# One batch's q transposed on TensorE instead of by DMA, the last quarter stored in two halves, and new instruction lists

## The chip, the core and the metric

The kernel runs on one NeuronCore of one Trainium2 chip. The time is device microseconds of one execution: 237.6 us is the median of three runs of the kernel before, which lie between 237.46 and 240.7 us. The profiled execution took 238.53 us, of which the span of its instructions is 236.7 us; the other 1.83 us lie outside the span.

## The reference

Eight batches of attention in two steps, followed by a gated MLP:

```python
s = scale * q k^T;  a = exp(s - max) / sum          # sm_attn(qq, kk, vv)
p_packed = sm_attn(p, k, v)          # 32 packed queries per head over 576 keys
out      = sm_attn(q, p_packed, p_packed)   # 576 queries over the 32 packed keys
x = out as (8*576, 8*64)
h = x @ w_in                          # 512 -> 2048
g = h * sigmoid(beta * h)
return g @ w_out                      # 2048 -> 512
```

Shapes: q, k, v (8, 8, 576, 64), p (8, 8, 32, 64), w_in (512, 2048), w_out (2048, 512), output (4608, 512), all float32 outside; the kernel computes in bfloat16 with float32 sums.

## The kernel before

The work goes batch by batch (b = 0 to 7). For each batch q, k and v are loaded by SyncE's queue, cast to bfloat16, and k and q are transposed, since both are contracted over the head dimension. In batches 0 and 1 (`PE_BATCHES = 2`) the transposes run on TensorE into PSUM (`tp`, L424) and VectorE or ScalarE copy them out (L585, L587, L608, L610); from batch 2 on one DMA transpose per tensor (L597) writes kT and qT directly, once all three casts of the tensor are done.

Then come the first scores (`s1`, `s1r`) and their exponential, the packed values (`pun`, tile `pp_ps`), the second scores (`s2`), exponential, sum over 32 keys (`z2`), its inverse by log and exp on ScalarE (`l2`, `n2`), and the weights `A2T` on VectorE (L890). The packed values are multiplied with w_in (`w`, tile `w_ps`), scaled by beta on VectorE (`W_bf`, L950 and L957). The hidden layer is then `h` = W_bf times A2T, two matmuls of 512 columns for each of 16 slices of the hidden dimension, then silu on ScalarE (`g_main`, L992). The 64 leftover tokens of a batch (576 = 512 + 64) go into `hr` and are collected over four batches in `g_rem`.

The last product is `o`: for batch 0 plain, 64 pairs of 512-column matmuls; for the others by a scheme with seven products of half-size blocks in place of eight (`plan_seven`, `seven`): four sums of g on VectorE (`S`, tile `g_sum`, L1223), seven products `p`/`P` of 16 matmuls with 256 columns each, reads `R11` to `R22+` from PSUM into `o_sb` (L1253, L1255), and stores (L1155). The sums of w_out blocks that it needs (`T4`, tile `w_sum`, L1133) are made once, after all of w_out is there.

Loads at the start share one ring of three staging buffers: w_in 0 to 3, w_out 0 to 3 and the packed queries p of batches 2 to 7 (L1414) go through it, and each must wait until the casts from the buffer's previous tenant are done. p is cast on POOL (L1418) and transposed on TensorE (`p_tr`, tile `pT_ps`), ahead of the first scores of batch 2.

What sets the order: five written lists (`SEQUENCE`, L84), one for each engine, give the order of all tasks; a table `HOME` says which PSUM ring some early tiles take. `Planner.run` walks these lists with assumed durations only to decide which engine's next task is emitted and how many filler matmuls (`keep_warm`, L438: 128x128 on a matrix of ones) stand before a TensorE task in the first 60 us. Each engine's order is then fixed in the program, and the engines wait for each other by semaphores alone. Where one TensorE instruction waits, all behind it wait.

Of the kernel before, what the change touches and what calls it, by code (L numbers as in the profile page):

```python
# [25 lines left out]
TS = 9  # L26
# [36 lines left out]
HOME = {  # L63
    ("bcol",): "att",
    ("brow", 0): "att",
    ("brow", 1): "att",
    ("brow", 3): "att",
    ("tr", 0, "k", 0): "h",
    ("trr", 0, "k"): "h",
    ("tr", 0, "q", 0): "h",  # L70
    ("tr", 0, "q", 1): "h",
    ("s1r", 0): "h",
    ("z2", 0, 1): "h",
    ("z2", 0, 2): "h",
    ("w", 0, 0): "h",
    ("w", 0, 2): "h",
    ("tr", 1, "k", 0): "h",
    ("trr", 1, "q"): "h",
    ("s1r", 1): "h",
    ("z2", 1, 0): "h",  # L80
    ("w", 1, 0): "h",
# [1470 lines left out]
```

## Time and profile before

| What | Value |
|---|---|
| median of 3 runs | 237.6 us (237.46 to 240.7) |
| profiled execution, its span | 238.53 us, 236.7 us |
| TensorE busy | 226.3 us (96%), 2642 matmuls |
| VectorE, ScalarE, POOL busy | 158.5 us, 169.6 us, 70.9 us |
| granted TensorE clock | full speed in all 40 slices |
| chain that ended last | 75% TensorE, 14% DMA |

The page's busy shares are means over the span; a row of a window tells what is busy in one stretch. In the chain of waits, each piece is what released the next one. In the timeline a number in brackets is the engine's idle time before the instruction, followed by what ended it.

### The profile page before, as it was taken

How to read it: one execution, taken by the hardware profiler on the slowest of the kernel's cores; microseconds unless marked ns; L12 is line 12 of the kernel's file. 1: busy time of each engine (PE TensorE's matmuls, PEld its weight loads, DVE VectorE, ACT ScalarE, POOL GpSimd, SP SyncE). 2: the span in 40 equal slices, each digit the busy share in tenths (PEclk: the TensorE clock that was granted, in tenths of full speed). 3: DMA queues.
4: the chain of work that ended last, by engine and by line, in shares of the span. 5: the costliest groups of instructions: out<-in, count | busy, mean ns of one | idle time of the engine just before them, and what ended most of it. 6: DMA issues, size and time to landing. Idle time of an engine off the chain costs nothing.

```text
span 236.7 us, 6282 instructions
## 1 busy us (share of the span) xinstructions
PE 226.3 (96%) x2642; PEld 157.4 (67%) x2668; DVE 158.5 (67%) x255; ACT 169.6 (72%) x312; POOL 70.9 (30%) x84
## 2 busy tenths in 40 slices
PE   7999999969999999999999999999999999999993
PEld 7668743334577656865688557776685667777882
DVE  3755989688689627965786877913885657644661
ACT  2548889748799877985779669797898688665200
POOL 3557316411854052046108420813305000000000
PEclk9999999999999999999999999999999999999999
DMA  6999999999998899999999999799893340031313
GB/s 227 395 387 399 395 395 332 280 333 221 275 274 170 238 250 204 284 295 252 254 280 342 203 290 242 186 295 214 166 322 58 60 172 8 4 136 44 82 54 133
DMA packets 67108, 54.16 MB, mean 229 GB/s; under 512 B 38948, under 2 KB 58532, under 8 KB 66568
## 3 DMA queue, kind: packets, MB, share of 16 engines
q1 hardware_dynamic: 67072, 53.75, 84.6%
q8 instruction: 21, 0.34, 0.6%
q14 instruction: 7, 0.06, 0.1%
q10 hardware_dynamic: 8, 0.01, 0.0%
HBM read 37.23 MB, written 9.44 MB: 197 GB/s over the span
## 4 chain that ended last, share of the span: by engine, by line
PE 75%; DMA 14%; SPq 2%; DVE 2%; POOL 2%; ACT 1%; issue 1%; POOLq 0%; ACTq 0%
PE o_ps L419 44%; PE h_ps L419 19%; DMA w_in<-in_moe_w_in_dram 5%; DMA w_out<-in_moe_w_out_dram 5%; PE hr_ps L419 3%; DMA v<-in_v_dram 3%; PE w_ps L419 3%; PE s_ps L419 2%; DMA k<-in_k_dram 2%; PE pp_ps L419 1%; PE z_ps L419 1%; POOL w_in_bf L1458 1%; SPq L483 1%; DVE g_main L1223 1%; SPq L490 1%
## 5 line engine op out<-in xcount | busy, mean ns | idle before, releaser
L992 ACT ACTIVATE g_main<-h_ps 128x512 bf16<-128x512 f32 x128 | 71.1, 595 | 32.4 <-PE h_ps L419 23.6
L419 PEld LDWEIGHTS <-g_main 128*128 128x128 bf16 x624 | 59.0, 98 | 22.0 <-issue 3.2
L419 PE MATMUL h_ps<-A2T,W_bf 128*128 128x512 bf16 x235 | 65.5, 379 | 0.7 <-issue 0.2
L419 PE MATMUL o_ps<-w_out_bf,g_main 128*128 128x256 bf16 (+1 forms) x395 | 59.9, 289 | 1.0 <-DVE o_sb L1255 0.5
L419 PEld LDWEIGHTS <-W_bf 128*128 128x128 bf16 x512 | 32.6, 98 | 19.5 <-issue 3.7
L950 DVE TENSOR_TENSOR W_bf<-w_ps,beta_bc 128x512 bf16<-128x512 f32 x48 | 30.5, 683 | 11.0 <-PE w_ps L419 10.8
L419 PE MATMUL o_ps<-w_sum,g_sum 128*128 128x256 bf16 x256 | 34.3, 273 | 0.1
L419 PE MATMUL o_ps<-w_sum,g_main 128*128 128x256 bf16 x224 | 30.4, 273 | 0.2
L436 ACT ACT_TABLE_LOAD x22 | 28.2, 1283 | 1.1 <-PEq L1536 0.7
L1253 DVE TENSOR_TENSOR o_sb<-o_ps,o_sb 128x512 f32<-128x512 f32 (+1 forms) x27 | 17.0, 629 | 17.9 <-PE o_ps L419 15.1
L419 PEld LDWEIGHTS <-g_sum 128*128 128x128 bf16 x256 | 24.0, 98 | 7.1 <-issue 1.7
L515 POOL CAST v_bf<-v 128x1024 bf16<-128x1024 f32 x12 | 15.3, 1296 | 40.5 <-DMA v<-in_v_dram 35.7
L515 POOL CAST q_bf<-q 128x1024 bf16<-128x1024 f32 x12 | 13.6, 1150 | 28.2 <-DMA q<-in_q_dram 15.7
L1255 DVE COPY o_sb<-o_ps 128x512 f32<-128x512 f32 (+1 forms) x21 | 13.1, 624 | 10.6 <-PE o_ps L419 8.7
L1255 ACT COPY o_sb<-o_ps 128x512 f32<-128x512 f32 (+1 forms) x15 | 8.2, 546 | 15.3 <-PE o_ps L419 15.3
L515 POOL CAST k_bf<-k 128x1024 bf16<-128x1024 f32 x12 | 13.2, 1123 | 13.2 <-DMA k<-in_k_dram 6.6
L419 PE MATMUL o_ps<-ones 128*128 128x128 bf16 x176 | 14.5, 238 | 1.1 <-DVE ones L1302 1.1
L419 PEld LDWEIGHTS <-ones 128*128 128x128 bf16 x176 | 12.2, 108 | 3.1 <-issue 1.2
L957 DVE SCALAR_TENSOR_TENSOR W_bf<-w_ps,rz,beta_bc 128x512 bf16<-128x512 f32 x16 | 11.3, 742 | 1.8 <-PE w_ps L419 1.6
L890 DVE TENSOR_TENSOR A2T<-E2T,rz 128x512 bf16<-128x512 bf16 x16 | 11.2, 709 | 0.6 <-ACT rz L885 0.6
L1223 DVE TENSOR_TENSOR g_sum<-g_main 128x2048 bf16<-128x2048 bf16 x7 | 8.8, 1256 | 3.3 <-ACT g_main L992 3.3
L419 PE MATMUL w_ps<-w_in_bf,pp 64*32 64x512 bf16 x256 | 10.7, 382 | 0.1
(124 smaller groups left out, 269.7 us busy)
## 6 DMA issues: line engine op xcount, KB each, us to landing
k<-in_k_dram SPq DMA_DIRECT2D x6, 1024.0 KB, 8.9
v<-in_v_dram SPq DMA_DIRECT2D x6, 1024.0 KB, 8.2
q<-in_q_dram SPq DMA_DIRECT2D x6, 1024.0 KB, 8.8
out_dram<-o_sb SPq DMA_DIRECT2D x10, 512.0 KB, 4.5
w_in<-in_moe_w_in_dram SPq DMA_DIRECT2D x4, 1024.0 KB, 11.5
w_out<-in_moe_w_out_dram SPq DMA_DIRECT2D x4, 1024.0 KB, 11.1
out_dram<-o_sb SPq DMA_DIRECT2D x12, 256.0 KB, 4.5
k<-in_k_dram SPq DMA_DIRECT2D x4, 576.0 KB, 5.8
```

Source lines behind the costliest of these rows:

```text
L419: return self.nc.tensor.matmul(out, lhsT, rhs, start=start, stop=stop, tile_position=pos, skip_group_check=True)
L436: self.nc.scalar.preload_act_table_set(SETS[mode])
L483: nc.sync.dma_start(t[64 * g : 64 * g + 64, :].rearrange("p (h d) -> p h d", h=4), src[b, 4 * g : 4 * g + 4, SM:S, :].rearrange("h p d -> ...
L490: nc.sync.dma_start(t[:].rearrange("p (i e f) -> p i e f", i=2, e=2)[:, i], src[b].rearrange("(e i a) (s t) d -> i (a s) e (t d)", e=2, i= ...
L515: self.copy[engine](o[:, 0 : 32 * e].rearrange("p (t h e) -> p h t e", t=4, h=8)[:, h, :, 0:D], t[:, 0:2048].rearrange("p (h t d) -> p h t ...
L890: nc.vector.tensor_tensor(part(st[b, "A2"], i), part(st[b, "E2"], i), st[b, "rz2"][:, i] if i < 2 else st[b, "rz2r"][:], ALU.mult)
L950: nc.vector.tensor_tensor(st[b, "W"][:, r, cols].rearrange("q (f p) -> q f p", f=4), st[b, "w", m][:].rearrange("q (p f) -> q f p", f=4), ...
L957: nc.vector.scalar_tensor_tensor(st[b, "W"][:, r, cols].rearrange("q (f p) -> q f p", f=4), st[b, "w", m][:].rearrange("q (p f) -> q f p", ...
L992: nc.scalar.activation(st[b, "g"][:, ft, :], st[b, "h", ft][:], AF.Silu)
L1223: nc.vector.tensor_tensor(o, x, y, op)
L1253: nc.vector.tensor_tensor(o, x, o, ALU.add)
L1255: self.copy[engine](o, x)
```

## The change

Three edits, and all five lists written anew. q of batch 2 is transposed on TensorE (`ON_PE`), by two sets of eight and one of two 128x128 transposes with three copies out of PSUM; its DMA transpose goes away. In the last unit the last quarter of the output (`R21`) is read and stored by halves of its tokens: the first half does not wait for the last group of matmuls. Beside the order itself, the lists give 15 tasks from ScalarE to VectorE and 16 the other way; eight casts and one cross copy (`pn` of batch 0) leave POOL for VectorE or ScalarE, and one cross copy comes to it (`pn` of batch 1).

```diff
 PE_BATCHES = 2
+ON_PE = ((2, "q"),)
 ...
 HOME = {
+    ("p0_tr",): "h",
 ...
-        return [("pun", b)] if x == "v" else [("tr", b, x, 0), ("tr", b, x, 1)] + [("trr", b, x)] * (b < PE_BATCHES)
+        return [("pun", b)] if x == "v" else [("tr", b, x, 0), ("tr", b, x, 1)] + [("trr", b, x)] * (b < PE_BATCHES or (b, x) in ON_PE)
 ...
-                a = 128 * (TS * i + t)
+                a = 128 * ((TS if b < PE_BATCHES else 8) * i + t)
 ...
-            if x == "k":
+            if x == "k" or b >= PE_BATCHES:
 ...
-                a = 128 * (TS * u + 8)
+                a = 128 * (TS * u + 8 if b < PE_BATCHES else 16 + u)
 ...
-            if b >= PE_BATCHES:
+            if b >= PE_BATCHES and (b, x) not in ON_PE:
 ...
-            for row, col in ((0, 0), (1, 1), (0, 1), (1, 0)):
+            for m in range(2):
+                self.task(("store", n + 1, 0, m), "SP", 0.36, lambda m=m: store(1, 0, slice(m, m + 1)), [c["21"][m]], -10)
 ...
+            for row, col in ((0, 0), (1, 1), (0, 1)):
 ...
-        c21 = R("21", [p4, r22], ends=[one])
+        if b == B - 1:
+            c21 = [
+                self.task(
+                    ("R21", b, m), {"DVE": 0.38, "ACT": 0.28}, None, lambda e, m=m: read("21", e, m),
+                    [p4 if m else ("p", b, 4, 2), r22], base + 5, ends=[one] if m else (),
+                )
+                for m in range(2)
+            ]
+        else:
+            c21 = R("21", [p4, r22], ends=[one])
```

SyncE's queue, the loads behind those of batch 0. Before (the k of the first line is batch 1's, k_732 batch 2's, and the p near the end holds the packed queries of batches 2 to 7):

```order
L490 DMA k_215<-in_k_dram 128x2x576 x2
L1452 DMA w_in_238<-in_moe_w_in_dram 128x4x512
L1452 DMA w_in_247<-in_moe_w_in_dram 128x4x512
L1462 DMA w_out_253<-in_moe_w_out_dram 128x2048
L1452 DMA w_in_634<-in_moe_w_in_dram 128x4x512
L1452 DMA w_in_727<-in_moe_w_in_dram 128x4x512
L475 DMA k_732<-in_k_dram 128x8x256
L483 DMA k_732<-in_k_dram 64x4x64 x2
L1462 DMA w_out_836<-in_moe_w_out_dram 128x2048
L1414 DMA p_865<-in_p_dram 96x1024
L1462 DMA w_out_916<-in_moe_w_out_dram 128x2048
```

Now (the first line is the first w_in; q_789 and k_888 belong to batch 2):

```order
L1465 DMA w_in_176<-in_moe_w_in_dram 128x4x512
L489 DMA k_216<-in_k_dram 128x2x576 x2
L1465 DMA w_in_237<-in_moe_w_in_dram 128x4x512
L489 DMA q_312<-in_q_dram 128x2x576 x2
L1475 DMA w_out_357<-in_moe_w_out_dram 128x2048
L1465 DMA w_in_613<-in_moe_w_in_dram 128x4x512
L1465 DMA w_in_778<-in_moe_w_in_dram 128x4x512
L474 DMA q_789<-in_q_dram 128x8x256
L1475 DMA w_out_846<-in_moe_w_out_dram 128x2048
L1427 DMA p_871<-in_p_dram 96x1024
L474 DMA k_888<-in_k_dram 128x8x256
L1475 DMA w_out_926<-in_moe_w_out_dram 128x2048
```

The first w_in stands ahead of k of batch 1 instead of behind it, each load of w_in by itself; q of batch 2 has taken the place of k of batch 2, and k of batch 2 stands behind p and ahead of the last w_out.

VectorE around the first scaled weights of batch 0 (`W_bf`, the first SCALAR_TENSOR_TENSOR). Before:

```order
L610 COPY kT<-krT_ps 128x256
L608 COPY qT<-qrT_ps 128x2x2x64
L585 COPY kT<-kT_ps 128x1024
L890 TENSOR_TENSOR A2T<-E2T,rz_458 128x512
L957 SCALAR_TENSOR_TENSOR W_bf<-w_ps,rz_364,beta_bc 128x512 x2
L890 TENSOR_TENSOR A2T<-E2T,rz_458 128x512
L1469 TENSOR_SCALAR w_out_bf<-w_out_253,rbeta 128x512
L957 SCALAR_TENSOR_TENSOR W_bf<-w_ps,rz_364,beta_bc 128x512
```

Now:

```order
L607 COPY qT<-qrT_ps 128x2x2x64
L1413 COPY beta_bc<-brow_ps 128x512
L776 COPY pp<-px 64x64 x2
L530 CAST k_bf<-k_216 128x2x9x64
L956 SCALAR_TENSOR_TENSOR W_bf<-w_ps,rz_359,beta_bc 128x512 x2
L584 COPY kT<-kT_ps 128x1024
L889 TENSOR_TENSOR A2T<-E2T,rz_469 128x512 x2
L609 COPY kT<-krT_ps 128x256
L584 COPY kT<-kT_ps 128x1024
L1471 CAST w_in_bf<-w_in_237 128x2x512
```

The cross copy of the packed values (`pp<-px`) and a cast of k of batch 1 have come from POOL and stand ahead of the first W_bf; the transposed k of batch 1 (`kT`) is copied out behind it instead of ahead of it, and a cast of w_in has come in.

TensorE around the transposes of p (`pT_ps`, eight of them; the first and the last are shown). Before:

```order
L419 LDWEIGHTS W_bf
L419 MATMUL h_ps<-A2T,W_bf 128x512
L424 LDWEIGHTS p_865
L424 MATMUL pT_ps<-identr,p_865 128x96
...
L424 LDWEIGHTS p_865
L424 MATMUL pT_ps<-identr,p_865 128x96
L419 LDWEIGHTS W_bf
L419 MATMUL h_ps<-A2T,W_bf 128x512
...
L419 LDWEIGHTS ones
L419 MATMUL o_ps<-ones 128x128
```

Now:

```order
L418 LDWEIGHTS W_bf
L418 MATMUL h_ps<-A2T,W_bf 128x512
L418 LDWEIGHTS g_main
L418 MATMUL o_ps<-w_out_bf,g_main 128x512
L418 LDWEIGHTS g_main
L418 MATMUL o_ps<-w_out_bf,g_main 128x512
L423 LDWEIGHTS p_871
L423 MATMUL pT_ps<-identr,p_871 128x96
...
L423 LDWEIGHTS p_871
L423 MATMUL pT_ps<-identr,p_871 128x96
L418 LDWEIGHTS W_bf
L418 MATMUL h_ps<-A2T,W_bf 128x512
```

Ahead of these transposes stand now 22 pairs of h matmuls instead of 19, 17 pairs of o matmuls instead of 15, the two new sets of eight q transposes, and all 170 fillers (before: 164 ahead, 12 behind, 176 in all); the first pair of o that reads the ninth and tenth slice of w_out stands ahead of them, too.

## Rows read from the trace of the kernel before

**Rows 1.** the page's part 1, busy time, share and instructions of each engine.

```profile
PE 226.3 (96%) x2642; PEld 157.4 (67%) x2668; DVE 158.5 (67%) x255; ACT 169.6 (72%) x312; POOL 70.9 (30%) x84
```

**Rows 2.** the page's part 4, shares of the chain that ended last.

```profile
PE 75%; DMA 14%; SPq 2%; DVE 2%; POOL 2%; ACT 1%; issue 1%; POOLq 0%; ACTq 0%
```

**Rows 3.** stretches: start:end, length, each engine's busy time (instructions), clock, DMA share, GB/s.

```profile
45.00:50.00 5.00, 2.84 (x13) 1.08 (x11) 3.06 (x7) 2.77 (x5) 1.06 (x2) 1.00 0.98 285
...
25.00:45.00 20.00, 19.63 (x214) 9.11 (x216) 18.95 (x35) 17.52 (x29) 8.36 (x8) 1.00 1.07 359
...
60.00:233.00 173.00, 170.97 (x2004) 124.03 (x2022) 114.64 (x171) 128.18 (x236) 45.27 (x51) 1.00 0.80 194
...
22.82:64.01 41.19, 38.52 (x374) 19.66 (x378) 34.22 (x57) 32.38 (x58) 17.07 (x18) 1.00 1.08 323
```

**Rows 4.** timeline: start, us, engine, line, operation, out<-in, idle before <-releaser.

```profile
37.82 0.36 SPq L1414 DMA_DIRECT2D p<-in_p_dram  x1
...
48.94 1.04 POOL L1418 CAST p<-p 96x1024 bf16<-96x1024 f32 x1 [3.92 <-DVE W_bf L957]
...
50.04 0.51 PE L424 MATMUL pT_ps<-identr,p 96*128 96x96 bf16 x8 [2.19 <-POOL p L1418]
...
51.25 1.28 DVE L1469 TENSOR_SCALAR w_out_bf<-w_out,rbeta 128x512 bf16<-128x512 f32 x3 [0.39 <-DMA w_out<-in_moe_w_out_dram]
```

**Rows 5.** issues on SyncE's queue: KB each, median us to landing.

```profile
p<-in_p_dram SPq DMA_DIRECT2D x1, 384.0 KB, 11.0
```

**Rows 6.** pieces of the chain: start, us, what.

```profile
8.33 11.36 DMA w_in<-in_moe_w_in_dram
...
19.81 2.49 POOL w_in_bf L1458 x2
...
28.09 0.45 PE qT_ps L424 x8
...
53.38 0.43 PE o_ps L419 x2
```

**Rows 7.** timeline, a run of fillers on TensorE.

```profile
23.06 1.18 PE L419 MATMUL o_ps<-ones 128*128 128x128 bf16 x18
```

**Rows 8.** timeline, VectorE's first W_bf and first sum of g.

```profile
22.82 1.41 DVE L957 SCALAR_TENSOR_TENSOR W_bf<-w_ps,rz,beta_bc 128x512 bf16<-128x512 f32 x2 [1.42 <-PE w_ps L419]
...
64.01 1.29 DVE L1223 TENSOR_TENSOR g_sum<-g_main 128x2048 bf16<-128x2048 bf16 x1
```

**Rows 9.** timeline, VectorE operations of the kinds added or removed.

```profile
19.98 0.69 DVE L585 COPY kT<-kT_ps 128x1024 bf16<-128x1024 bf16 x1 [0.17 <-PE kT_ps L424]
...
20.59 0.81 DVE L890 TENSOR_TENSOR A2T<-E2T,rz 128x512 bf16<-128x512 bf16 x1
...
19.32 0.29 DVE L610 COPY kT<-krT_ps 128x256 bf16<-128x256 bf16 x1 [0.98 <-PE krT_ps L424]
...
36.20 0.69 DVE L1458 CAST w_in_bf<-w_in 128x1024 bf16<-128x1024 f32 x1
...
30.98 0.76 DVE L531 CAST v_bf<-v 128x1152 bf16<-128x1152 f32 x1 [0.18 <-DMA v<-in_v_dram]
...
24.92 0.48 DVE L1469 TENSOR_SCALAR w_out_bf<-w_out,rbeta 128x512 bf16<-128x512 f32 x1
...
34.01 0.38 DVE L777 COPY pp<-px 64x64 bf16<-64x64 bf16 x2
...
54.73 0.56 DVE L1426 COPY pT<-pT_ps 64x384 bf16<-64x384 bf16 x1
```

**Rows 10.** timeline of ScalarE, a table load and what follows it.

```profile
34.17 1.28 ACT L436 ACT_TABLE_LOAD   x1
...
35.47 1.26 ACT L849 ACTIVATE E2T<-s_ps,rz 128x512 bf16<-128x512 f32 x2
```

**Rows 11.** timeline, ScalarE's reads of output blocks near the end.

```profile
219.91 0.37 ACT L1255 COPY o_sb<-o_ps 128x256 f32<-128x256 f32 x1 [0.22 <-PE o_ps L419]
...
233.01 0.58 ACT L1255 COPY o_sb<-o_ps 128x512 f32<-128x512 f32 x1 [9.85 <-PE o_ps L419]
```

More of the change, by code (lines that the diff above doesn't have):

```diff
@@ L66 @@
     ("brow", 1): "att",
[L67 to L70, printed above, removed]
+    ("brow", 2): "att",
     ("tr", 0, "q", 1): "h",
-    ("s1r", 0): "h",
+    ("trr", 0, "q"): "h",
+    ("s1", 0, 0): "h",
     ("z2", 0, 1): "h",
-    ("z2", 0, 2): "h",
     ("w", 0, 0): "h",
-    ("w", 0, 2): "h",
-    ("tr", 1, "k", 0): "h",
+    ("w", 0, 1): "h",
     ("trr", 1, "q"): "h",
-    ("s1r", 1): "h",
+    ("s2", 1, 1): "h",
     ("z2", 1, 0): "h",
-    ("w", 1, 0): "h",
 }
@@ L85 @@
     "PE": [
[69 rows of a table removed]
[70 rows of a table added]
         ("p", "r1", 4, 0), ("P", "r1", 4), ("p", "r1", 3, 0), ("P", "r1", 3), ("p", 7, 1, 0), ("p", 7, 1, 1),
[4 rows of a table removed]
[4 rows of a table added]
     ],
     "ACT": [
[37 rows of a table removed]
[38 rows of a table added]
     ],
     "DVE": [
[5 rows of a table removed]
-        ("w_out", 7), ("W", 1, 0), ("w_in", 2, 1), ("take", 0, 0), ("W", 1, 1), ("take", 0, 2), ("W", 0, 4),
-        ("W", 0, 5), ("W", 1, 2), ("A2", 1, 0), ("W", 1, 3), ("A2", 1, 1), ("W", 1, 4), ("W", 1, 5), ("W", 0, 6),
-        ("W", 0, 7), ("w_out", 10), ("w_out", 8), ("W", 1, 6), ("W", 1, 7), ("take", 0, 1), ("w_out", 11),
-        ("w_out", 9), ("w_out", 13), ("w_out", 15), ("w_out", 12), ("take", 0, 3), ("T4", 1), ("pT1", 0, 0),
[22 rows of a table removed]
[6 rows of a table added]
+        ("px", 1), ("w_out", 6), ("w_out", 5), ("w_out", 4), ("w_out", 7), ("W", 1, 0), ("w_in", 2, 0),
[25 rows of a table added]
     ],
     "POOL": [
-        ("p0_bf",), ("cast", 0, "q", 0), ("cast", 0, "v", 0), ("cast", 0, "v", 1), ("cast", 1, "k", 0),
-        ("cast", 1, "k", 1), ("pn", 0), ("w_in", 0, 1), ("w_in", 0, 0), ("w_in", 1, 1), ("w_in", 1, 0),
-        ("cast", 1, "q", 1), ("cast", 1, "v", 0), ("w_in", 2, 0), ("w_in", 3, 1), ("w_in", 3, 0), ("cast", 2, "k", 0),
-        ("cast", 2, "k", 1), ("cast", 2, "k", 2), ("p_bf",), ("cast", 2, "q", 0), ("cast", 2, "q", 1),
[10 rows of a table removed]
+        ("cast", 0, "q", 0), ("cast", 0, "v", 0), ("w_in", 0, 0), ("cast", 1, "k", 1), ("w_in", 1, 1), ("pn", 1),
+        ("w_in", 3, 0), ("w_in", 3, 1), ("cast", 2, "q", 0), ("cast", 2, "q", 1), ("p_bf",), ("cast", 2, "k", 0),
[11 rows of a table added]
     ],
     "SP": [
[14 rows of a table removed]
-        ("tr", 7, "q", 0), ("store", 11), ("store", 12), ("store", 14), ("store", 13), ("store", "r1", 0),
-        ("store", "r1", 1), ("store", 16, 0), ("store", 17, 1), ("store", 16, 1), ("store", 17, 0),
[14 rows of a table added]
+        ("store", 13), ("store", 14), ("store", "r1", 0), ("store", "r1", 1), ("store", 16, 0), ("store", 17, 1),
+        ("store", 16, 1), ("store", 17, 0, 0), ("store", 17, 0, 1),
     ],
@@ L606, in evacuate_rest @@
             ps = st[b, x, "rps"][:, 0:256]
-            if x == "q":
+            if x == "q" and b < PE_BATCHES:
                 self.copy[engine](by_head(b)[..., SM:S], ps.rearrange("p (i a s) -> p i a s", i=2, a=2))
@@ L625, in plan_attention @@
                     ("tr", b, x, i), "PE", (0.45, 0.15), lambda x=x, i=i: transpose(x, i),
-                    [("cast", b, x, i)] + old, rank, takes="att",
+                    [("cast", b, x, i)] + ([("cast", b, x, 0), ("cast", b, x, 1)] if b >= PE_BATCHES else []) + old, rank, takes="att",
                 )
@@ L633, in plan_attention @@
                 ("trr", b, x), "PE", (0.12, 0.15), lambda x=x: transpose_rest(x),
-                [("cast", b, x, 0), ("cast", b, x, 1), ("T", b, x, 0)] + old + [("s1r" if x == "k" else "none", b - 1)], rank + 1, takes="att",
+                [("cast", b, x, i) for i in range(2 if b < PE_BATCHES else 3)] + [("T", b, x, 0)] + old + [("s1r" if x == "k" else "none", b - 1)], rank + 1, takes="att",
             )
@@ L1145, in plan_seven, with store @@
         nc, st = self.nc, self.t
-        def store(row, col=None):
+        def store(row, col=None, m=slice(0, 2)):
             if b < PE_BATCHES:
@@ L1154, in store @@
             n = slice(0, DM) if col is None else slice(256 * col, 256 * col + 256)
-            nc.sync.dma_start(rows[:, :, n], st[b, "ob", row][:, :, n])
+            nc.sync.dma_start(rows[:, m, n], st[b, "ob", row][:, m, n])
         n = len(self.outs)
@@ L1169, in plan_seven @@
         else:
-            for row, col in ((0, 0), (1, 1), (0, 1), (1, 0)):
+            for m in range(2):
+                self.task(("store", n + 1, 0, m), "SP", 0.36, lambda m=m: store(1, 0, slice(m, m + 1)), [c["21"][m]], -10)
+            self.tk["store", n + 1, 0] = self.tk["store", n + 1, 0, 1]
+            for row, col in ((0, 0), (1, 1), (0, 1)):
                 self.task(("store", n + row, col), "SP", 0.72, lambda row=row, col=col: store(row, col), [c[f"{row + 1}{col + 1}"]], -10)
@@ L1244, in product, with read @@
                 )
-        def read(name, engine):
+        def read(name, engine, m=None):
             row, col = int(name[0]) - 1, int(name[1]) - 1
@@ L1251, in read @@
             x = st[b, "B" if name in ("11+", "22", "12+") else "A"][:, 0 : 256 * M].rearrange("p (m n) -> p m n", m=M)
+            if m is not None:
+                o, x = o[:, m], x[:, m]
             if name[2:]:
```

329 rows, old and new, of the table SEQUENCE are left out of this document.

## The prediction

> **What bounds the kernel now.** I read the page's busy shares first, then the chain of waits, then the busy times by stretch, and in the stretches that are not full the timeline. The shares name TensorE, with 226.3 us of work in a span of 236.7 [rows 1], and the chain says the same for three quarters of its length, with transfers as the second entry [rows 2]. Both are means. The stretches tell where something is to be had: from 60 to 233 us TensorE is without work for 173.00 - 170.97 = 2.0 us in all, so nothing that only reorders that part can bring much. In 45 to 50 us it is idle for 2.16 of 5 us [rows 3]. The timeline has that hole as one wait: the transposes of p wait 2.19 us for POOL's cast of p, which itself starts 0.1 us after p lands (issued at 37.82, 11.0 us to landing) [rows 4, 5]. Ahead of it the head of the kernel hangs on loads: the first w_in lands at 19.7 us, and POOL's two casts of it take 2.49 us more [rows 6]; the DMA engines are full there. And VectorE is busy for 18.95 of the 20 us from 25 to 45 [rows 3]: it is the second bound, hidden under TensorE.
>
> **The change part by part.** The sum is made against the profiled execution, 238.53 us; the median of the runs shown, 237.6, is 0.93 lower, and I take that off at the end.
>
> *The transposes of q of batch 2.* They add 18 transposes of 128x128. A set of eight takes 0.45 us in the chain, 0.056 us each [rows 6], so 18 x 0.056 = +1.0 us on TensorE, all of it on the path, since TensorE is the path. The Trainium skill (VectorE: DVE Perf Modes, "The three transpose paths") gives 390 ns for one on TensorE; by that the 18 would be 7.0 us, an estimate, and the forecast 6 us higher; the row is the same operation in a run and decides. The DMA transpose that goes was off the path. What it leaves is room in SyncE's queue for the loads of batch 3, and since TensorE is full from 60 us on, I cost that at nothing.
>
> *The wait for p.* Ahead of p's transposes there is now more work: three h pairs and two o pairs at 0.43 us, two sets of q transposes at 0.45, six more fillers at 1.18 / 18 = 0.066 us [rows 6, 7], together 2.15 + 0.90 + 0.39 = 3.4 us against a wait of 2.19. p itself is issued when its staging buffer is free (the casts of the third w_in), which does not move by the lists alone; ahead of it the queue carries q instead of k of batch 2 without its small rest, 0.13 MB less. So p comes at the same time, TensorE later, and the wait goes: -2.19 us. The other end is 0, if TensorE is held elsewhere; it is kept for the range.
>
> *Fillers.* 170 instead of 176: six at 0.066 = -0.4 us. They stand in place of waits, so nearer to 0 if a wait is there anyway.
>
> *The end.* The last read of ScalarE, 0.58 us for two blocks of 256 columns, starts when the last matmul is done; now only one block is left for it then, 0.37 us [rows 11]: -0.2 us. The store behind it moves half the bytes; SyncE issues one more, during the last four matmuls. I add nothing for either.
>
> *New waits.* The load of k of batch 2 (128 x 8 x 256 float32, 1.05 MB) now runs ahead of the last w_out, the small rest (0.13 MB) behind: 0.92 MB more ahead, at the 359 GB/s of 25 to 45 us [rows 3] 2.6 us. Today that w_out is there at 51.25 us, where VectorE waits 0.39 us for it [rows 4]. The pairs of o that read it, the sums of w_out behind it, and the first scores of batch 2 (kT now comes later by the same shift) can each wait up to that. Bounds 0 and 2.6; I take 0.8, twice the pause of today: the change moves pairs of h and o ahead of p that give these loads time, but it does not move them by 2.6 us.
>
> *ScalarE* gets two more table loads around the first hidden slices (ScalarE's list goes back to the exponential and out again), 2 x 1.28 = 2.6 us [rows 10]. It has 20 - 17.52 = 2.5 us to spare in 25 to 45 us [rows 3], and TensorE has fillers there: I take 0; 2.6 is the other end. The Trainium skill (ScalarE: Activation LUTs, "What ACT_TABLE_LOAD costs") has 1.28 us for the load and 1.38 us of drain on top; by it the pair would be 5.3 us, an estimate, and would no longer fit; the trace does not agree, the exponential starts 0.02 us behind the load's end.
>
> *VectorE.* Ahead of its first sum of g it gets what follows. Between the first W_bf and that sum there are new: four copies of transposes (0.69 each), one A2T (0.81), one small copy (0.29), two casts of w_in (0.69), two of q and v (0.76), two of w_out (0.48): 2.76 + 0.81 + 0.29 + 1.38 + 1.52 + 0.96 = 7.7 us; gone are a cross copy (0.38), a cast of w_in (0.69), a copy of pT (0.56): 1.6. Net +6.1 us [rows 9]. Against it, the first W_bf comes earlier: today it waits for w_ps [rows 8], that is for w_in, and w_in now stands ahead of k of batch 1 (1.18 MB, 3.3 us at 359 GB/s), and its two casts run on two engines instead of one after the other (half of 2.49): 3.3 + 1.2 = 4.5 us, so 18.3 us instead of 22.82. From there VectorE needs 34.22 + 6.1 = 40.3 us [rows 3]: 58.6 us plus waits, against 64.01 today [rows 8]. It keeps its place as long as it waits under 5.4 us on the way; today it waits 41.19 - 34.22 = 7.0 us, half of which is for TensorE and loads that come earlier or are not waited for when it has other work. I take 0.
>
> Sum: 238.53 + 1.0 - 2.19 - 0.4 - 0.2 + 0.8 = 237.5; less 0.93: **236.6 us**.
>
> **The rivals.**
>
> *VectorE becomes the bound, slower.* The place is 18 to 64 us. If all 7.0 us of today's waits stay, the first sum of g starts at 18.3 + 40.3 + 7.0 = 65.6, 1.6 us late; if the first W_bf does not come earlier either, at 70.1, 6.1 us late. It decides from 5.4 us of waits on. What is late there is late at the end, since nothing behind it has slack. At 3 us, and without the other terms (what TensorE saves ahead of that point is lost in waiting): 238.53 + 3 - 0.2 - 0.93 = 240.4 us. For it: 95% busy in 25 to 45. Against: 13% idle behind that, and casts on POOL that no longer get in its way. The Trainium skill (Perfetto Trace Analysis, "Optimizing Scalar/DVE Operations") advises to take work off a saturated VectorE; this change puts work on it, and by that advice this rival is the likely one. The trace bears it out for 25 to 45 us only.
>
> *The wait only changes its place.* The hole at p closes and one of the same size opens at the last w_out or at kT of batch 2: 238.53 + 1.0 - 0.4 - 0.2 - 0.93 = 238.0 us. For it: 2.6 us of shift in those loads. Against: TensorE reads them 3.4 us of work later than it did p.
>
> *The head gains more.* No new waits, and half of the 4.5 us by which the first W_bf comes earlier is kept to the end: 236.6 - 0.8 - 2.2 = 233.6 us. For it: the chain runs through that load [rows 6]. Against: the loads behind it are not earlier, and the hidden layer cannot run past w_out.
>
> **How the numbers follow.** Forecast 0.42, wait in another place 0.25, VectorE 0.18, head 0.15. The forecast's own range is 235.6 to 237.6. To hold 8 in 10, the range takes in the wait in another place, and about half each of the head's case and of VectorE's: 234.2 to 239.8. A measurement of this kernel can tell about 2% from no change: below 232.8 or above 242.4 us. Only the upper part of the head's case (0.04) and the far end of VectorE's (0.03) lie there; within 2%: 0.93.
>
> **What would show it.** Right: no idle TensorE ahead of the transposes of p; the first W_bf near 18.3 us; the first sum of g at 62 to 64 us; the gap between TensorE's last matmul and ScalarE's last end at 0.4 us instead of 0.6. Wrong: VectorE full and TensorE waiting for W_bf or a sum of g between 40 and 70 us; TensorE waiting for the last w_out's casts or for kT; a first W_bf that is still at 22 us; or holes behind 70 us that no row of today shows, since the lists are new there, too.

## The result, and the profile after

The changed kernel takes **236.01 us** (median of 7 runs, 235.84 to 236.94), the kernel before 238.14 beside it (7 runs, 237.46 to 240.7). The ratio is **0.990** (95% interval 0.986 to 0.994): about 1% faster, within 2%. Forecast were 236.6 us, 234.2 to 239.8, and no change over 2%.

The profiled execution takes 236.20 us with a span of 234.3 (before 238.53 and 236.7). Three points divide the difference. The first scores of batch 2 start 1.11 us earlier on TensorE (62.09, before 63.20). From there to the end of the last matmul it takes 168.59 us, 1.19 less than before (230.68 and 232.98 are the ends). Behind the last matmul to the end of the span it is 3.6 instead of 3.7. These are single executions; how firm the 1.19 us are is taken up with e5.

The busy times of the engines, beside [rows 1]:

```profile
PE 226.7 (97%) x2653; PEld 158.2 (68%) x2680; DVE 163.8 (70%) x266; ACT 174.3 (74%) x316; POOL 62.7 (27%) x75
```

The same work of TensorE, 0.4 us more of it, in a shorter span: what went is idle time. The stretches, columns as in [rows 3], show where:

```profile
45.00:50.00 5.00, 5.00 (x48) 2.50 (x48) 4.61 (x9) 4.07 (x8) 1.04 (x1) 1.00 1.10 326
50.00:55.00 5.00, 4.57 (x27) 2.12 (x27) 3.45 (x8) 3.75 (x8) 2.31 (x3) 1.00 1.08 287
25.00:45.00 20.00, 19.45 (x214) 9.92 (x216) 17.80 (x34) 18.12 (x31) 5.27 (x6) 1.00 1.04 369
60.00:231.00 171.00, 169.48 (x2000) 123.27 (x2018) 115.09 (x168) 128.47 (x240) 44.20 (x47) 1.00 0.75 194
```

From 45 to 50 us TensorE is full (2.84 of 5 in [rows 3]); from 50 to 55 a small hole is new; VectorE has more room from 25 to 45 than before, not less; and behind 60 us TensorE is without work for 1.5 us instead of 2.0, 0.3 of them behind its last matmul. TensorE's timeline in the round of p, columns as in [rows 4]:

```profile
47.88 0.61 PE L423 MATMUL qT_ps<-identr,q_bf 128*128 128x128 bf16 x8
...
49.26 0.61 PE L423 MATMUL qT_ps<-identr,q_bf 128*128 128x128 bf16 x8
...
51.00 0.51 PE L423 MATMUL pT_ps<-identr,p 96*128 96x96 bf16 x8
...
54.45 0.38 PE L418 MATMUL o_ps<-w_out_bf,g_main 128*128 128x512 bf16 x1 [0.36 <-DVE w_out_bf L1482]
...
62.09 0.28 PE L418 MATMUL s1r_ps<-pT,kT 128*128 128x128 bf16 x2
```

p's transposes stand a microsecond later than in [rows 4] and wait for nothing; the two sets of q transposes are ahead of them; the new wait is for the last w_out. VectorE at the places of [rows 8], and at that w_out:

```profile
17.07 1.27 DVE L776 COPY pp<-px 64x64 bf16<-64x64 bf16 x2
18.77 0.76 DVE L530 CAST k_bf<-k 128x1152 bf16<-128x1152 f32 x1 [0.42 <-DMA k<-in_k_dram]
19.44 1.40 DVE L956 SCALAR_TENSOR_TENSOR W_bf<-w_ps,rz,beta_bc 128x512 bf16<-128x512 f32 x2
...
53.91 0.88 DVE L1482 TENSOR_SCALAR w_out_bf<-w_out,rbeta 128x512 bf16<-128x512 f32 x2 [1.55 <-DMA w_out<-in_moe_w_out_dram]
...
62.58 1.46 DVE L1225 TENSOR_TENSOR g_sum<-g_main 128x2048 bf16<-128x2048 bf16 x1
```

The first W_bf comes 3.4 us earlier and the first sum of g 1.4 us, though VectorE is busy for 38.90 of the 43.14 us from the one to the other (34.22 of 41.19 in [rows 3]). The end, where [rows 11] has one read of 0.58 us (here the timelines of TensorE and ScalarE):

```profile
228.77 1.91 PE L418 MATMUL o_ps<-w_sum,g_main 128*128 128x256 bf16 x16
...
230.72 0.65 ACT L1259 COPY o_sb<-o_ps 128x256 f32<-128x256 f32 x2 [6.40 <-PE o_ps L418]
```

Both half reads start only behind the last matmul (228.77 + 1.91 = 230.68). The waits of TensorE behind 60 us in the kernel **before** (who waits <- for whom, us, times, longest) are gone in the changed one:

```profile
PE o_ps L419 <- DVE o_sb L1255: 0.5, 1, 0.5
PE pp_ps L419 <- POOL v_bf L515: 0.3, 1, 0.3
PE h_ps L419 <- issue: 0.2, 1, 0.2
```

### The profile page after: what moved, and what is told of

It reads as the page before. It is cut to its first block, busy times and chain, and to the rows that moved or that the text cites. A ratio compares the mean times of both kernels' runs of the same rounds, so it can differ in the third digit from the quotient of the medians.

```text
span 234.3 us, 6327 instructions
## 1 busy us (share of the span) xinstructions
PE 226.7 (97%) x2653; PEld 158.2 (68%) x2680; DVE 163.8 (70%) x266; ACT 174.3 (74%) x316; POOL 62.7 (27%) x75
## 4 chain that ended last, share of the span: by engine, by line
PE 79%; DMA 14%; ACT 2%; SPq 2%; issue 1%; POOL 1%; DVE 0%; ACTq 0%; POOLq 0%
PE o_ps L418 47%; PE h_ps L418 19%; DMA w_in<-in_moe_w_in_dram 9%; DMA w_out<-in_moe_w_out_dram 5%; PE hr_ps L418 3%; PE w_ps L418 3%; PE s_ps L418 2%; PE z_ps L418 1%; SPq L489 1%; PE pp_ps L418 1%; POOL w_in_bf L1471 1%; ACT g_main L991 1%; PE kT_ps L423 0%; PE qT_ps L423 0%; PE s1r_ps L418 0%
## 5 line engine op out<-in xcount | busy, mean ns | idle before, releaser
L418 PE MATMUL o_ps<-w_out_bf,g_main 128*128 128x256 bf16 (+1 forms) x398 | 61.1, 289 | 0.5 <-DVE w_out_bf L1482 0.4
L418 PE MATMUL o_ps<-w_sum,g_sum 128*128 128x256 bf16 x256 | 33.6, 273 | 0.1
L418 PE MATMUL o_ps<-w_sum,g_main 128*128 128x256 bf16 x224 | 31.0, 273 | 0.3
L418 PEld LDWEIGHTS <-g_sum 128*128 128x128 bf16 x256 | 24.5, 98 | 6.9 <-issue 1.1
L1259 ACT COPY o_sb<-o_ps 128x512 f32<-128x512 f32 (+1 forms) x19 | 9.4, 498 | 14.6 <-PE o_ps L418 14.6
L1259 DVE COPY o_sb<-o_ps 128x512 f32<-128x512 f32 (+1 forms) x18 | 11.8, 658 | 11.9 <-PE o_ps L418 11.7
L514 POOL CAST q_bf<-q 128x1024 bf16<-128x1024 f32 x12 | 12.5, 1057 | 27.5 <-DMA q<-in_q_dram 26.1
L514 POOL CAST k_bf<-k 128x1024 bf16<-128x1024 f32 x12 | 12.3, 1044 | 15.0 <-DMA k<-in_k_dram 9.8
L889 DVE TENSOR_TENSOR A2T<-E2T,rz 128x512 bf16<-128x512 bf16 x16 | 12.8, 822 | 1.4 <-ACT rz L884 1.2
```

What stands on the lines that cost most here:

```text
L418: return self.nc.tensor.matmul(out, lhsT, rhs, start=start, stop=stop, tile_position=pos, skip_group_check=True)
L514: self.copy[engine](o[:, 0 : 32 * e].rearrange("p (t h e) -> p h t e", t=4, h=8)[:, h, :, 0:D], t[:, 0:2048].rearrange("p (h t d) -> p h t ...
L889: nc.vector.tensor_tensor(part(st[b, "A2"], i), part(st[b, "E2"], i), st[b, "rz2"][:, i] if i < 2 else st[b, "rz2r"][:], ALU.mult)
L1259: self.copy[engine](o, x)
```

## The experiments

Twelve kernels ran, each beside the kernel before, in four groups on four chips. That kernel spreads by 4 us, in part for a reason that matters here: in 27 of its 98 executions beside these twelve the mean granted clock of TensorE was 0.990 to 0.993, with a median of 240.19 us; in the other 71, called **full clock** below, it was 0.996 or more, with a median of 238.23 us. So each result has both: the median of all, and the count of executions below 0.996 with the median at full clock. "First scores" is the start of the first scores of batch 2 in the profiled execution, "rest" the time from there to the end of the last matmul.

| kernel | median us (runs) | ratio to before, 95% | below 0.996 | full clock | first scores | rest |
|---|---|---|---|---|---|---|
| before | 238.14 (7) | 1 | 27 of 98 | 238.23 | 63.20 | 169.78 |
| changed | 236.01 (7) | 0.990, 0.986 to 0.994 | 0 of 7 | 236.01 | 62.09 | 168.59 |
| e1 | 239.48 (12) | 1.002, 0.999 to 1.005 | 5 of 12 | 238.72 | 65.17 | 169.28 |
| e2 | 236.71 (6) | 0.990, 0.986 to 0.994 | 0 of 6 | 236.70 | 61.73 | 169.55 |
| e3 | 236.31 (4) | 0.989, 0.984 to 0.994 | 0 of 4 | 236.31 | 62.10 | 168.58 |
| e4 | 235.83 (10) | 0.990, 0.986 to 0.994 | 0 of 10 | 235.83 | 61.67 | 169.38 |
| e5 | 237.97 (12) | 0.994, 0.991 to 0.998 | 0 of 12 | 237.97 | 62.88 | 168.62 |
| e6 | 238.26 (12) | 0.996, 0.993 to 0.999 | 0 of 12 | 238.26 | 63.16 | 169.69 |
| e7 | 238.87 (12) | 0.999, 0.995 to 1.003 | 8 of 12 | 237.35 | 62.88 | 168.60 |
| e8 | 238.19 (12) | 0.996, 0.992 to 0.999 | 1 of 12 | 237.93 | 61.33 | 170.19 |
| e9 | 238.69 (12) | 1.000, 0.996 to 1.004 | 3 of 12 | 238.54 | 62.65 | 169.11 |
| e10 | 237.70 (12) | 0.998, 0.996 to 1.001 | 0 of 12 | 237.69 | 62.90 | 169.72 |
| e11 | 237.28 (12) | 0.994, 0.991 to 0.997 | 0 of 12 | 237.28 | 63.03 | 168.62 |
| e12 | 235.87 (6) | 0.989, 0.985 to 0.993 | 0 of 6 | 235.87 | 61.78 | 169.32 |

Executions of one kernel at full clock differ by 1 to 2 us in most rows (2.8 in e4, 3.6 in before), so differences of under half a microsecond between medians, or under one between two profiled executions, are not read as effects by themselves. The kernel before has a median at full clock of 238.20 to 238.44 us in each of the four groups, so medians at full clock are compared across them.

### e1 and e2: the lists spliced at 62 us

The edits put one kernel's lists ahead of the first scores of batch 2 and the other's behind, on all five engines:

```diff
 e1: "PE", "ACT", "DVE", "POOL", "SP":
-    [changed, to ("s1", 2, 0)] + [changed, behind it]
+    [before, to ("s1", 2, 0)] + [changed, behind it]
 e2:
+    [changed, to ("s1", 2, 0)] + [before, behind it]
```

> The lists of the kernel before up to the second half of the first scores of batch 2 (about 62 us), those of the changed kernel behind it; q of batch 2 goes by DMA, and the last quarter is read and stored whole. It tells where the 1.2 us came from that the changed kernel gains behind 62 us (230.68 - 62.09 = 168.59 us from there to the last matmul, before 232.98 - 63.20 = 169.78). If from the new order of the lists behind 62 us: 1.2 us below the kernel before, and the waits for o_sb (0.5 us) and for v_bf (0.3 us) that the trace of before has there are gone. If from what the head hands over (q of batch 2 off SyncE's queue, loads of batch 3 earlier): the time of the kernel before, within 0.4 us, with those waits or others like them.

> The other half: the lists of the changed kernel up to about 62 us, with q of batch 2 transposed on TensorE, and those of the kernel before behind it; the last quarter by halves of tokens. If each part keeps its own gain: the first scores of batch 2 at 62.1 us as in the changed kernel, 168.6 + 1.2 us from there to the last matmul, so 1.1 us below the kernel before. If the gain behind 62 us comes from the head: 2.1 to 2.3 us below it, as the changed kernel.

The new lists behind 62 us gained nothing on the old head: e1 is at 238.72 us at full clock, so the theory that each part keeps its own gain fell there. The old lists behind the new head, e2, keep most of the gain: 236.71, 1.5 us below the kernel before and between the two forecasts (1.1, and 2.1 to 2.3). But its profiled execution has that gain in the head (61.73) and a rest of 169.55, near that of before: that the head hands over a gain behind 62 us is not shown by e2. The new lists may not be without use: with both, another 0.7 us (236.01), and e2's trace still has a wait for o_sb (0.9 us) that the changed kernel lacks.

The profiled execution of e1 showed what nobody had forecast. TensorE waits for p, and the clock falls behind that wait. Its row, then its stretches (length, busy time of TensorE, its loads, VectorE, ScalarE, GpSimd, **granted clock**, DMA share, GB/s):

```profile
50.34 0.51 PE L424 MATMUL pT_ps<-identr,p 96*128 96x96 bf16 x8 [2.51 <-POOL p L1418]
...
45.00:50.00 5.00, 2.83 (x13) 1.07 (x11) 3.02 (x6) 2.77 (x5) 0.91 (x2) 1.00 1.00 278
50.00:51.00 1.00, 0.66 (x9) 0.54 (x11) 0.99 (x3) 0.00 (x0) 0.29 (x1) 1.00 1.05 360
51.00:52.00 1.00, 0.95 (x5) 0.43 (x5) 0.49 (x2) 0.67 (x2) 0.00 (x0) 0.64 1.08 350
52.00:53.00 1.00, 1.00 (x12) 1.00 (x10) 0.79 (x2) 1.00 (x2) 0.00 (x0) 0.50 1.10 350
53.00:54.00 1.00, 1.00 (x6) 0.45 (x5) 0.00 (x0) 0.02 (x1) 0.00 (x0) 0.50 1.09 348
54.00:55.00 1.00, 1.00 (x5) 0.39 (x4) 0.04 (x1) 0.00 (x0) 0.00 (x0) 0.66 1.12 354
55.00:60.00 5.00, 5.00 (x25) 2.29 (x24) 4.53 (x6) 4.00 (x8) 1.70 (x2) 1.00 1.27 189
```

Right behind the hole ahead of p's transposes (2.51 us here) the clock falls to 0.50, 1.2 GHz, and comes back before 55 us. Added up over the four rows, 0.36 + 0.50 + 0.50 + 0.34, TensorE loses 1.7 us: about the 2.0 us between the two groups of executions of before. That made the hole the thing to test, with e5 to e7.

### e3 and e4: the end

```diff
 e3 (changed kernel, the last quarter whole again)
-        ("R21", 7, 0), ("R21", 7, 1),      ("store", 17, 0, 0), ("store", 17, 0, 1),
+        ("R21", 7),                        ("store", 17, 0),
 ...
 e4 (changed kernel, side A of the last unit in two banks)
+            own = b == B - 1 and side == "A" and m == 1
+            if own and i == 1 and half == 0:
+                st[b, "A1"] = self.ps_h.tile([128, 512], f32, tag="h", name="h_ps")
-            out = st[b, side][:, 256 * m : 256 * m + 256]
+            out = st[b, "A1"][:, 0:256] if own else st[b, side][:, 256 * m : 256 * m + 256]
 ...
```

> The changed kernel with the last quarter read and stored whole again, its lists otherwise as they are. My theory now: in the changed kernel both half reads start only behind the last matmul (230.72 us), so the edit gained nothing: the time of the changed kernel within 0.2 us, and ScalarE ends 0.5 to 0.7 us behind TensorE's last matmul in both. The prediction on record: 0.2 us longer, ScalarE 0.6 us behind the last matmul here and 0.4 us there.

> The changed kernel, with the last unit's side A in two banks of PSUM, one for each half of the tokens; three reads of that side are two instructions each. If the first half read is held because its tile also takes the last matmuls: now it starts before the last matmul is done, only the second is left behind it, ScalarE ends 0.35 to 0.45 us behind the last matmul instead of 0.69, and the time is 0.2 to 0.3 us below the changed kernel. If it is held by something else (the order in which the program is written, ScalarE itself): both reads behind the last matmul as now, no gain.

In e3 the one read of ScalarE starts where both halves of the changed kernel do:

```profile
230.72 0.59 ACT L1255 COPY o_sb<-o_ps 128x512 f32<-128x512 f32 x1 [6.40 <-PE o_ps L417]
```

In e4 (TensorE's last two groups, then ScalarE's reads) the first read runs beside the last matmuls, which now write another bank:

```profile
230.01 0.60 PE L418 MATMUL o_ps<-w_sum,g_main 128*128 128x256 bf16 x4
230.45 0.60 PE L418 MATMUL h_ps<-w_sum,g_main 128*128 128x256 bf16 x4
...
230.69 0.37 ACT L1266 COPY o_sb<-o_ps 128x256 f32<-128x256 f32 x1 [6.22 <-PE o_ps L418]
231.09 0.37 ACT L1266 COPY o_sb<-h_ps 128x256 f32<-128x256 f32 x1
```

ScalarE ends 231.46 - 231.05 = 0.41 us behind TensorE, as expected, against 231.37 - 230.68 = 0.69 in the changed kernel and 0.63 in e3. So it was the shared tile that held the first half read; the tile is one bank, and which of the two holds it e4 cannot part. The 0.28 us do not show in the time (235.83 against 236.01, both within each other's spread). The Trainium skill (PSUM — Partial Sum Buffer, "PSUM bank collisions raise a hardware error") has a rule that bears on this: a read must be kept off a bank while a matmul writes into it, by bank and not by address. By it the halves of one bank could not overlap; both traces agree.

### e5 and e6: the hole ahead of p, closed in two ways

Both are the kernel before with one edit:

```diff
 e5, "PE":
-        ("p_tr",), ("h", 0, 14), ("h", 1, 9), ... ("h", 1, 4), ("o", 0, 1, 9), ("h", 1, 2),
+        ("h", 0, 14), ("h", 1, 9), ... ("h", 1, 4), ("o", 0, 1, 9), ("p_tr",), ("h", 1, 2),
 e6, transpose() of p:
             self.p_ps = ps = self.att("pT_ps", bf16)
+            for _ in range(34):
+                self.mm(ps.bitcast(f32)[:, 0:128], self.ones[:], self.ones[:])
```

> The kernel before with one entry moved in TensorE's list: the transposes of p behind the eight pairs of h and o (3.4 us) that stood behind them; nothing else. My theory: the hole ahead of p's transposes (2.19 us in the trace of before, 2.51 in the run with the head of before) is what the changed kernel saves in the head, twice: the wait itself, and in about a quarter of the executions of before a granted clock of 0.5 for 3.4 us right behind the hole (1.7 us more). So here no hole over 0.5 us, no execution with a mean clock below 0.996, 236.2 to 236.8 us: most of the gain by this one entry. Rival, the wait only changes place: a hole of the same size at the last w_out or at the reads of p, and the time of the kernel before within 0.4 us.

> The kernel before with 34 filler matmuls of 128x128 (0.0585 us each, 2.0 us) written into p's own bank of PSUM ahead of its transposes: the pairs behind still wait for p, but TensorE has work in the hole. It parts the two costs of the hole. If the low clock comes from the hole: no execution below 0.996 any more, and the time is that of the executions of before at full clock (median 238.2, none above 239.7). If the low clock comes from elsewhere (the chip, not the program): as with the kernel before, about 6 of 23 executions at 0.992 or 0.993, 240 to 241 us.

Neither had an execution below 0.996 in 12, where before has 27 of 98 (13 of 35 beside these two). In e6 nothing else is gained: 238.26 us, that of before at full clock. TensorE's rows:

```profile
47.74 2.06 PE L419 MATMUL pT_ps<-ones 128*128 128x128 bf16 x34
...
50.00 0.51 PE L424 MATMUL pT_ps<-identr,p 96*128 96x96 bf16 x8 [0.20 <-POOL p L1418]
```

So filling the hole takes the low clock away. But e5, where p is not waited for at all, is only 0.26 us below before at full clock: my theory of 236.2 to 236.8 us fell, and the rival came true. TensorE in e5, then the wait of VectorE that it hangs on:

```profile
50.33 0.83 PE L419 MATMUL o_ps<-ones 128*128 128x128 bf16 x12 [1.18 <-DVE o_sb L1054]
...
53.84 0.50 PE L424 MATMUL pT_ps<-identr,p 96*128 96x96 bf16 x8
...
62.88 0.28 PE L419 MATMUL s1r_ps<-pT,kT 128*128 128x128 bf16 x2
...
47.47 0.88 DVE L1469 TENSOR_SCALAR w_out_bf<-w_out,rbeta 128x512 bf16<-128x512 f32 x2 [1.94 <-DMA w_out<-in_moe_w_out_dram]
```

The wait went to VectorE's read of an output tile, which stands behind a wait of VectorE of 1.94 us for the third w_out.

The rest of e5 matters for another question. It is 168.62 us, as short as in the changed kernel, and neither the wait for o_sb nor that for v_bf is there, though e5 has the lists of before behind 62 us and q of batch 2 by DMA. This execution (236.98 us) is 1 us below the median of e5. And e4, the changed kernel but for its last unit, has a rest of 169.38. So the rest differs by 0.8 to 1.2 us between single executions of kernels with the same lists behind 62 us, and the 1.19 us between before and changed are not shown to be an effect of the change.

### e7: the hole put into the changed kernel

```diff
 "PE":
-        ("w", 1, 3), ("h", 1, 4), ... ("h", 1, 10), ("o", 0, 1, 9), ("p_tr",),
+        ("w", 1, 3), ("p_tr",), ("h", 1, 4), ... ("h", 1, 10), ("o", 0, 1, 9),
```

> The changed kernel with one entry moved in TensorE's list: the transposes of p ahead of seven pairs and the two sets of q transposes (3.9 us) that stood ahead of them. p is there at 49.0 to 49.2 us, TensorE then at 47.1: a hole of about 2 us again. My theory: 1.9 us slower than the changed kernel at full clock (238.1), and again some executions with a mean clock of 0.993 and about 2 us more. Rival, the hole was hidden: the time of the changed kernel within 0.4 us.

```profile
48.40 0.51 PE L423 MATMUL pT_ps<-identr,p 96*128 96x96 bf16 x8 [1.47 <-POOL p L1431]
```

The hole is back, 1.47 us in this execution, and with it the low clock: 8 of 12 executions, 239.25 us in the median, 1.9 more than the other four. At full clock it costs 237.35 - 236.01 = 1.3 us; the first scores start 0.79 later and the rest is as before (168.60).

### e8: q of batch 2 by DMA again

```diff
-ON_PE = ((2, "q"),)
+ON_PE = ()
 ...
 "SP":
-        ("tr", 2, "k", 0), ("ld", 3, "k", 0),
+        ("tr", 2, "k", 0), ("tr", 2, "q", 0), ("ld", 3, "k", 0),
```

> The changed kernel with q of batch 2 transposed by DMA again (behind k's on SyncE's queue), and the 18 transposes, their copies and their places in the lists gone. The term in question is +1.0 us for the transposes on TensorE, against what SyncE's queue hands on: the loads of batch 3 come 4 us later. p's transposes come 0.9 us earlier and still find p there (slack 2.0 us). If the term holds and the queue is worth nothing: 0.8 to 1.0 us below the changed kernel. If the queue is what gave the gain behind 62 us: waits for v_bf, kT or qT between 62 and 100 us of 0.3 to 1.2 us, and the changed kernel's time or more.

The head is 0.76 us shorter, near the 0.9 us of the two sets, and the rest 1.60 us longer; in the time, 237.93 us at full clock against 236.01, and no execution of e8 is below the slowest of the changed kernel (237.1 and 236.94). The two longest of TensorE's three waits behind 62 us, then on SyncE's queue the transpose of q of batch 2 and the issues of batch 3:

```profile
76.47 0.29 PE L419 MATMUL s1r_ps<-pT,kT 128*128 128x128 bf16 x2 [0.32 <-DMA kT<-k_bf]
83.23 0.59 PE L419 MATMUL pp_ps<-v_bf,E1T 128*32 128x65 bf16 x38 [0.43 <-POOL v_bf L515]
...
58.81 2.75 SPq L597 DMA_TRANSPOSE qT<-q_bf  x1
61.61 0.58 SPq L475 DMA_DIRECT2D k<-in_k_dram  x1
...
70.88 3.55 SPq L597 DMA_TRANSPOSE kT<-k_bf  x1
74.48 0.58 SPq L475 DMA_DIRECT2D v<-in_v_dram  x1
```

The same three issues in the changed kernel:

```profile
59.17 0.52 SPq L474 DMA_DIRECT2D k<-in_k_dram  x1
...
68.00 4.41 SPq L596 DMA_TRANSPOSE kT<-k_bf  x1
72.45 0.58 SPq L474 DMA_DIRECT2D v<-in_v_dram  x1
```

The transpose holds SyncE's queue for 2.75 us; batch 3's k, its transpose and v go out 2.0 to 2.9 us later, and TensorE waits for k's transposed tile and for v's casts. In the kernel before, v of batch 3 goes out at 76.63 and TensorE waits 0.3 us for its cast. So in these lists the 1.0 us of transposes on TensorE buys more than it costs. That it does so through the queue is shown for these two waits, 0.75 us of the 1.60; e5 has the same transpose in the queue without them, so the way of the remainder is open.

### e9 to e12: what the head rests on, and two tries at better

```diff
 e9 (e5, and in "DVE"):
-        ("w_out", 10), ("w_out", 8), ("W", 1, 6), ("W", 1, 7), ("take", 0, 1),
+        ("W", 1, 6), ("W", 1, 7), ("take", 0, 1), ("w_out", 10), ("w_out", 8),
 e10 (e4, and in "SP"):
-        ("ld", 2, "k", 0), ("ld_out", 3),
+        ("ld_out", 3), ("ld", 2, "k", 0),
 e11 (changed, "SP"):
-        ("ld_in", 0), ("ld", 1, "k", 0), ("ld", 1, "k", 1),
+        ("ld", 1, "k", 0), ("ld", 1, "k", 1), ("ld_in", 0),
 e12 (e4, "SP"; p's cast, transposes and copies later on their engines, too):
-        ("ld", "p"), ("ld", 2, "k", 0), ("ld_out", 3),
+        ("ld", 2, "k", 0), ("ld_out", 3), ("ld", "p"),
```

> The kernel with p's transposes moved late in the lists of before (1.18 us of wait for VectorE's read of an output tile in the place of the hole), and two entries moved in VectorE's list: the first two casts of the third w_out behind two W_bf and that read. VectorE waited 1.94 us for that w_out ahead of work whose data were there. My theory: the wait that took the hole's place hung on VectorE's order and not on a transfer, so it goes: no wait over 0.4 us between 44 and 56 us, first scores of batch 2 at 61.6 to 61.9 us instead of 62.88, 236.6 to 237.0 us. Rival: it hangs on the load of w_out: the wait is then in front of the pair that reads w_out, 62.5 to 63 us at the first scores, and no gain beside the kernel without these two entries (237.97).

> A version meant to beat both: the changed kernel with side A of the last unit in two banks (0.28 us of the end in the run of that edit alone), and the load of the last w_out ahead of k of batch 2 on SyncE's queue. The wait for the last w_out in the changed kernel (0.36 us on TensorE and a slow pair behind it, 1.55 us on VectorE) should go; k's transposed tile comes up to 2.6 us later, at 60 to 61.5 us, and is needed at 61.2. If that is still in time: 0.6 to 1.0 us below the changed kernel, 235.0 to 235.4 us. If not: a wait for kT ahead of the first scores of batch 2, of the size of what was saved or more, 235.8 to 237 us.

> The changed kernel with one entry moved in SyncE's list: the first w_in behind both halves of k of batch 1, as in the kernel before. It tells what the earlier first w_in is worth (first W_bf at 19.44 instead of 22.82 us). If the head of the changed kernel rests on it: first W_bf at 21.5 to 22.5 us, waits on TensorE between 20 and 55 us, first scores of batch 2 at 63.5 to 64.5 instead of 62.1, 237.4 to 238.4 us. If the head hangs on the loads that come later (p, the last two w_out): k of batch 1 comes earlier, the head catches up, and the time is that of the changed kernel within 0.5 us.

> A second try at a version that beats both: side A of the last unit in two banks, and p loaded behind k of batch 2 and the last w_out instead of ahead of them, with its cast behind the two large casts of k, its transposes nine pairs later on TensorE and its four copies spread over the last slices of batch 1 on ScalarE. k and w_out come 0.4 MB earlier, 1.1 us at 359 GB/s. If that takes the wait for the last w_out away (0.36 us and a slow pair, 0.6 to 1.0 us in all) and p is still in time: first scores of batch 2 at 61.0 to 61.5 us, 235.0 to 235.5 us. If p is late: a wait ahead of its transposes of 0.5 to 2 us near 55 us, or ahead of the first scores, 236 to 238 us, and if it is over 1.5 us some executions at a low clock.

e9: the wait for VectorE's read near 50 us is gone, and the next one stands in front of a pair that reads w_out. There is another ahead of it, at 38 us:

```profile
38.39 0.59 PE L419 MATMUL o_ps<-w_out_bf,g_main 128*128 128x512 bf16 x2 [0.74 <-DVE o_sb L1054]
...
51.24 0.81 PE L419 MATMUL o_ps<-w_out_bf,g_main 128*128 128x512 bf16 x3 [0.41 <-DVE w_out_bf L1469]
...
62.65 0.27 PE L419 MATMUL s1r_ps<-pT,kT 128*128 128x128 bf16 x2
```

The rival held in the time: no gain from these two orders. The wait at 38 us lies ahead of the entries that were moved: VectorE's cast of w_in just before it takes 1.47 us there and 0.69 in e5, why is open. Three executions were below 0.996 though the profiled one has no hole over 0.74 us behind 18 us; why stays open.

e10: the wait for the last w_out is gone and k's transposed tile is late, the rival again, and dearer than I priced it (237.69 against at most 237):

```profile
62.90 0.29 PE L418 MATMUL s1r_ps<-pT,kT 128*128 128x128 bf16 x2 [1.96 <-DMA kT<-k_bf]
```

e11: with the first w_in where it was, the first W_bf is 2 us later (VectorE), and the first scores 0.94 (TensorE):

```profile
21.45 1.41 DVE L956 SCALAR_TENSOR_TENSOR W_bf<-w_ps,rz,beta_bc 128x512 bf16<-128x512 f32 x2 [3.15 <-PE w_ps L418]
...
63.03 0.28 PE L418 MATMUL s1r_ps<-pT,kT 128*128 128x128 bf16 x2
```

No wait on TensorE stands for what was lost; the planner put in 225 fillers where it has 170 in the changed kernel, so what is missing is filled, and a part of the loss may be these fillers themselves. 237.28 us, 1.3 above the changed kernel and 0.1 below the range that I gave to the theory: a good part of the gain rests on the first w_in, how much of it directly is open.

e12: the wait for w_out is gone, and p is late in its place; then TensorE waits for ScalarE's exponentials, whose table load comes 0.6 us later behind p's copies (61.74, in the changed kernel 61.15):

```profile
55.67 0.51 PE L423 MATMUL pT_ps<-identr,p 96*128 96x96 bf16 x8 [1.03 <-POOL p L1438]
...
64.92 0.50 PE L418 MATMUL pp_ps<-v_bf,E1T 128*32 128x65 bf16 x40 [0.67 <-ACT E1T L665]
```

235.87 us, between the ranges of its two cases and the changed kernel's time within what can be told. No version here beats it beyond that.

## Why the prediction was right, and where not

The forecast held the time, by 0.6 us, and the class; its sum was less good than that. Made against the profiled execution it said 237.5, and that execution took 236.20: 1.3 us too high. The 0.93 us taken off for the median made good half of it, and by chance: with more executions the kernel before had a median of 238.14, 0.39 below its profiled one.

*The transposes of q, +1.0.* The size was right: 0.46 and 0.44 us from the start of each set to the start of what follows, and two more later. **The step that failed is the next sentence, "I cost that at nothing"**, on the room in SyncE's queue. That TensorE is full behind 60 us does not make the room worthless: without it (e8) the changed kernel is 1.9 us slower at full clock, though TensorE has less to do, and TensorE waits for kT and for casts of v. [Rows 3] already had 2.0 us without work behind 60 us; I did not ask what they waited for, and 0.3 of it was v of batch 3. The 1.19 us that the changed kernel gains there were forecast as 0; whether they come from this room stays open, since e5 has as short a rest without it.

*The wait for p, -2.19.* It went, and TensorE's first scores come 1.11 us earlier, where the terms ahead of that point (+0.9, -2.19, -0.4, +0.8) make -0.9. But the reason was too simple. Late transposes of p alone are worth 0.26 us (e5): in the lists of before the rival "the wait only changes its place" is what happens, to VectorE's read and then to w_out (e9). The changed kernel has other work in the hole, and loses 1.3 us without it (e7). That it has this work because its first w_in and W_bf come earlier is what e11 points to and does not prove; the prediction had this under VectorE and costed it at nothing for TensorE. And the hole had a second price that no row of the one profiled execution could show, the clock: 2.0 us in 27 of 98 executions, none of 7 now, nor of the 20 of e2 to e4, which have the same head. In the mean of many executions that is 0.55 us more gain than at full clock (27 / 98 x 2.0).

*New waits, +0.8.* Right: 0.36 us of wait and a slow pair behind it. Such a wait stands among the prediction's own signs of being wrong, yet its sum allows for it. e10 gives the price of the other order of the two loads, 1.96 us, within the 2.6 us that bounded it.

*The end, -0.2.* Failed. The gap grew from 0.61 to 0.69 us, since the first half read waits for the tile that the last matmuls still write. So what stands under "The change", that the first half does not wait for the last group of matmuls, holds for the program's order and not for the execution. e3 shows that the edit is worth nothing that can be told, e4 that the mechanism was right for two banks.

*ScalarE and VectorE, 0.* Right. Behind 30 us TensorE waits for ScalarE nowhere, and for VectorE for one cast of v (0.2 us) and that of w_out; the first sum of g is at 62.58 us, in the range given. The first W_bf is at 19.44 and not 18.3: the cross copy that went from GpSimd to VectorE took 1.27 us there, against the 0.38 of [rows 9], and a cast of k with its wait of 0.42 us stands behind it. The rival in which VectorE is the bound was weaker than priced: its "13% idle behind that" is a misreading, VectorE was busy for 13.09 of the 19.01 us from 45 to 64.01 us before, so 31% idle.

## What to carry to other kernels

Where the bounding engine is full, ask what its small waits hang on before costing a freed queue at nothing: here 0.9 us of work put on the full engine bought more than its own length (1.9 us net, by taking it away again in e8). A wait that is closed by order alone can come up again at the next late load, as in e5, e9, e10 and e12, so follow the work back to the load that decides, and move that. And look at the spread of a kernel's executions beside its profile: a cost that comes in one of four is not in the one trace that was read.

## What the runs showed of the chip

A hole of 2.51 us on TensorE near 48 us was followed by 1.2 GHz (granted clock 0.50 in e1's rows), though TensorE had work again; the 1.7 us lost there are about 3.4 us at that level, an estimate. For the other executions only the mean clock is on record. It was low in 27 of 98 of before (a hole of 2.19 us in the profiled one), 5 of 12 of e1, 8 of 12 of e7 (1.47 us). With the hole filled by idle matmuls (e6) it was none of 12. A hole of 1.96 us at 61 us (e10), seen in its one profile, did it in none of 12, so its length alone does not decide. And one execution of 12 of e8 and three of 12 of e9 were low, whose profiles have no wait over 0.52 and 0.74 us behind 18 us and ahead of 62: so the hole ahead of p may not be the only thing that does it. What decides was not tried. The Trainium skill (TensorE: Matmul & The Clock Gate, "HAM oscillation — how this bites in real kernels") has waits for data as what sends TensorE back to the low clock; the rows of e1 and the counts of e6 and e7 agree, the run e10 shows a wait that does not.
